# Attention, a dense MoE layer and a routed MoE layer in one kernel: gathers of later experts' tokens moved from the heads of two experts to the blocks of the experts before them

## The chip, the cores and the metric

The kernel runs on one core of one Trainium2 chip, as one launch. The metric is device time in microseconds (us) of that core; lower is better. The time quoted is the median of three runs. One further run was profiled, and all rows below come from it.

## The reference

Three stages follow each other over 2304 tokens (4 batches of 576) of width 512. Only the third is touched here.

```
x = attention(q, k, v)              # block-causal, 8 heads of 64, blocks of 64
x = elu(x @ w_in) @ w_out           # dense layer, 512 -> 2048 -> 512

skip_score = x @ w_skip             # routed layer, 8 experts
do_compute = skip_score > 0
out = x.copy()
xc = x[do_compute]
logits = xc @ w_gate
e_idx = argmax(logits)
gate_w = softmax(logits)[e_idx]
for e in range(8):
    mask = e_idx == e
    h = max(xc[mask] @ w1[e], 0)
    y[mask] = gate_w[mask] * (h @ w2[e])
out[do_compute] = xc + y
```

How many tokens an expert has is only known on the chip. Weights of an expert are w1 (512 x 1024) and w2 (1024 x 512).

## The kernel before

Attention and the dense layer are written through a recorder (class `Recorder`) that lays out the order of every engine by a list schedule; they end at about 604 us of the profiled execution and stay as they are. What follows is the routed layer, expert after expert.

**Tokens.** The router writes a list of token numbers per expert. A *gather* (`gather_to(e, j)`) fetches block j of expert e, 128 tokens: POOL issues an indirect DMA from `pay_d` into one of three staging buffers (two in tile `gp0`, one in tile `gp1`; they are used in turn, by the counter `ng`), and SP then issues a DMA transpose from there to the place that the matmuls read (`place_of`): a half of `mxt0`, `mxt1`, `mxwo2` or `mxwo6`. The next gather into a staging buffer has to wait until the transpose out of it has landed. A *scatter* adds a block's 128 result rows to `out`: ACT writes the rows to the tile `o` (two halves, used in turn by block), and POOL issues an indirect DMA from there.

**Blocks.** `block` computes one block on TensorE (PE): 96 matmuls into `hp`, ReLU and a split into high and low halves on ACT and DVE, 24 or 48 matmuls into `y`. The first block of small experts has 64 tokens instead of 128.

**Experts.** `ORDER` is 0, 6, 4, 5; `first_tokens` runs an expert's first block (its *head*), and `more_tokens` runs each further block inside a branch on the expert's count of tokens, each branch nested in the one before it. Every engine takes each branch for itself. Blocks past the fourth would run in a loop (`the_rest`). The four experts of `LAST` (1, 2, 3, 7) come at the end, their first blocks together in `last_tokens`. With the inputs of this kernel the blocks that run are: expert 0 one, expert 6 three, expert 4 three, expert 5 two, and one for each of 1, 2, 3, 7. Where a block does not run, its engines jump past its code to the next expert. The names E6 j2 and so on below mean expert 6, third block (j counts from 0).

**Weights.** The table `PREP` says what is done for later experts beside each block: `l` and `m` load half an expert's weights (four loads of 512 KB on SP's queue; `l` ahead of the block's own work, `m` later), `s`, `c` and `p` are steps of scaling and splitting on ACT and DVE. "4:l2-1 m7-0" loads w2 of expert 2 and w1 of expert 7 beside the head of expert 4.

**Which gathers stand where** (line 1710 and line 1793). The table `GATHERS` puts gathers behind an expert's first block, in the recording of its head; `more_tokens` puts more into the second block (j = 1), ahead of that block's own work. Before the change the head of expert 4 issues five gathers: its own third block, both blocks of expert 5 that will run, and the blocks of experts 1 and 2. The head of expert 5 issues three: its own third block and the blocks of experts 3 and 7. The second block of either expert issues one, for the fourth block.

POOL and SP work through their instructions in program order, so an instruction that waits holds up all that stand behind it.

Of the kernel before, what the change touches and what calls it, by code (L numbers as in the profile page):

```python
# [347 lines left out]
def tile_kernel(ctx, tc, q, k, v, w_in, w_out, w_skip, w_gate, w1, w2, out):  # L348
    nc = tc.nc
# [9 lines left out]
    NS = NT // 128 + 1  # L359
# [866 lines left out]
    for b in range(B):  # L1226
        g0, g1 = ubase[b, 0], ubase[b, 1]
# [191 lines left out]
        advance()  # L1419


    TM = 512

# [83 lines left out]
    def prep_steps(e, which, wait=0.0):  # L1509
        P_ = functools.partial  # L1510
        return ([("stat", P_(stat_w, e, which, x)) for x in range(4)] + [("scale", P_(scale_w, e, which, wait))]
                + [("split", P_(split_p, e, 4 * which + x)) for x in range(4)])
# [7 lines left out]
    def load_half(e, which, at=0.0):  # L1520
        for x in range(4):
            load_w(8 * e + 4 * which + x, at)
# [20 lines left out]
    def part(n, i32=False):  # L1543
        t = lists[:, off[0]:off[0] + n]
        off[0] += n
        return t.bitcast(I32) if i32 else t
# [3 lines left out]
    ni = part(17, True)  # L1550
# [42 lines left out]
    def gather(ix, xT):  # L1593
        gp = GP[ng[0] % 3]
        ng[0] += 1
        rc.gpsimd.indirect_dma_start(out=gp, out_offset=None, in_=pay_d[:, :],
                                     in_offset=bass.IndirectOffsetOnAxis(ap=ix, axis=0), bounds_check=NT - 1, oob_is_err=False)
        rc.sync.dma_start_transpose(out=xT, in_=gp.bitcast(F16))
# [89 lines left out]
    C0 = [int(any(x == e for x, _ in AHEAD)) for e in range(E)]  # L1688
# [3 lines left out]
    LAST = [1, 2, 3, 7]  # L1692
    XP = {0: 1, 6: 2, 4: 0, 5: 1}

    def place_of(e, j):
        if e in LAST:
            i = LAST.index(e)
            h = (X2[2 - i // 2 * 2], i % 2) if j == 0 else (X2[1], 1) if j == 1 else (X2[3], j % 2)
        else:
            h = X2[XP[e] if j < 2 else 3], j % 2  # L1700
        return h[0][:, :, 128 * h[1]:128 * h[1] + 128]

    def gather_to(e, j):
        gather(gix[:, e, C0[e] + j:C0[e] + j + 1], place_of(e, j))

    def pre_gather(e):
        for j in range(2):
            gather_to(e, j)

    GATHERS = {0: [], 6: [(6, 2), (4, 0), (4, 1)], 4: [(4, 2), (5, 0), (5, 1), (1, 0), (2, 0)], 5: [(5, 2), (3, 0), (7, 0)]}  # L1710

    PREP = {int(e): [x.split() for x in h.split("|")] for e, h in (y.split(":") for y in (
        "6:l1-1 m2-0 c5-0 p5-0 s1-0|c5-1 p5-1|c1-0 s1-1,4:l2-1 m7-0 p1-0 c1-1|p1-1 s2-0|c2-0 s2-1,"
        "5:l7-1 m3-0 p2-0 c2-1|p2-1,8:l3-1 s7-0 s7-1 c7-0 p7-0 c7-1 p7-1").split(","))}

    def aside_of(e, part):
        return PREP.get(e, [])[part:part + 1]
# [6 lines left out]
    def split_beside(e, part):  # L1724
        for h in sum(aside_of(e, part), []):
            if h[0] == "m":
                load_half(int(h[1]), int(h[3]), 5.0)
            if h[0] in "lm":
                continue
            for kind, f in prep_steps(int(h[1]), int(h[3]), 13.0 if e == 8 else 3.0):  # L1730
                if kind[1] == {"s": "t", "c": "c", "p": "p"}[h[0]]:
                    rc.atom()
                    rc.shift = -150000 if kind == "scale" else 0
                    f()
                    if h[0] == "s":
                        rc.ready[len(rc.steps) - 1] = 4.0
                    rc.shift = 0

    def tokens(e, j, xT, fs, par=None):

        c = C0[e] + j
        if j == 0 and e in SMALL:
            block(e, xT[:, :, 64:128], hix[:, e, c:c + 1], half[:, e, c, 1:2], j if par is None else par, 64)
        else:
            block(e, xT, six[:, e, c:c + 1], fs[:, c:c + 1], j if par is None else par)

    def first_tokens(e, fs):

        rc.begin()
        rc.late = rc.left  # L1750
        rc.urgent = True
        load_beside(e, 0)
        tokens(e, 0, place_of(e, 0), fs)
        rc.urgent = False
        for g in GATHERS[e]:
            gather_to(*g)
        split_beside(e, 0)
        rc.issue()

    def last_tokens():  # L1760

        rc.begin()
        rc.late = rc.left
        load_beside(8, 0)
        split_beside(8, 0)
        rc.urgent = True
        fs = {e: fac_w(e) for e in LAST}
        for i, e in enumerate(LAST):
            tokens(e, 0, place_of(e, 0), fs[e], i)
        rc.urgent = False  # L1770
        rc.issue()
        rc.left = {}
        with tc.If(cnt["last"] > 128, preferred_fallthrough_block=True, label="last"):  # L1773
            for e in LAST:
                read_count(e)
                more_tokens(e, 1, fs[e])

    def hint(e, j, n):

        tc.mark_branch_hint_location(f"n{e}_{j}", n > 128 * j, engines=[mybir.EngineType.PE])  # L1780

    def more_tokens(e, j, fs):

        aside = j and aside_of(e, j)
        now = rc.left
        keep = list(FREE), dict(RAW2), dict(WHL)
        with tc.If(cnt[e] > 128 * j, preferred_fallthrough_block=True, label=f"n{e}_{j}") as cmp:  # L1787
            if j < TM // 128:
                hint(e, j + 1, cnt[e])
                rc.begin()  # L1790
                rc.late = rc.left if j else {}
                rc.urgent = True
                for x in ((1, 2, 3) if e in LAST or e == 0 else (3,)) if j == 1 else ():
                    gather_to(e, x)
                tokens(e, j, place_of(e, j), fs)
                rc.urgent = False
                if aside:
                    split_beside(e, j)
                rc.issue()
                now = rc.left  # L1800
                more_tokens(e, j + 1, fs)

            else:
                the_rest(e, fs)
        if aside:
            with cmp.Else():
                FREE[:] = keep[0]
                for x, y in ((RAW2, keep[1]), (WHL, keep[2])):
                    x.clear()
                    x.update(y)  # L1810
                rc.begin()
                for part in range(j, len(PREP[e])):
                    split_beside(e, part)
                rc.issue()
        if j == 1:
            rc.left = now

    def the_rest(e, fs):

        trips = nc.values_load(ni[0:1, 8 + e:9 + e], min_val=TM // 128, max_val=NS)  # L1820
        sel = sm.tile([128, 3, NS], F32, tag="rw", bufs=1, name="sel")
        cj = sm.tile([128, 4], F32, tag="mx", bufs=4, name="cj")
        ci_ = sm.tile([128, 2], I32, tag="si", bufs=1, name="cji")
        nc.vector.memset(cj[:, 0:1], float(C0[e] + TM // 128 - 1))
        nc.gpsimd.iota(sel[:, 0], pattern=[[1, NS]], base=0, channel_multiplier=0, allow_small_or_imprecise_dtypes=True)
        with tc.For_i(TM // 128, trips):
            nc.vector.tensor_scalar(out=cj[:, 0:1], in0=cj[:, 0:1], scalar1=1.0, scalar2=None, op0=ALU.add)
            nc.vector.tensor_scalar(out=sel[:, 1], in0=sel[:, 0], scalar1=cj[:, 0:1], scalar2=None, op0=ALU.is_equal)
            for x, src in ((1, gix[:, e, :]), (2, six[:, e, :]), (3, fs)):
                nc.vector.tensor_tensor(out=sel[:, 2], in0=sel[:, 1], in1=src, op=ALU.mult)  # L1830
                nc.vector.tensor_reduce(out=cj[:, x:x + 1], in_=sel[:, 2], axis=AX.X, op=ALU.add)
            nc.vector.tensor_copy(ci_, cj[:, 1:3])
            gather(ci_[:, 0:1], X2[3][:, :, 0:128])
            block(e, X2[3][:, :, 0:128], ci_[:, 1:2], cj[:, 3:4], 0)
# [75 lines left out]
    with tc.manual_schedule():  # L1910
        for i, e in enumerate(ORDER):
            fs = fac_w(e)
            if i:
                hint(e, 1, cnt[e])
            first_tokens(e, fs)
            if i:
                read_count(ORDER[i + 1] if i + 1 < len(ORDER) else "last")
            n0 = ng[0]
            more_tokens(e, 1, fs)
            ng[0] = n0  # L1920
            FREE.extend(WHL.pop(8 * e + x) for x in range(8))
        tc.mark_branch_hint_location("last", cnt["last"] > 128, engines=[mybir.EngineType.PE])
        last_tokens()
# [23 lines left out]
```

## Time and profile before

| | us |
|---|---|
| median of three runs | 736.51 (735.89 to 737.37) |
| the profiled execution | 733.4 |
| its span, first to last instruction | 731.4 |
| expert 6, three blocks (604.25 to 637.01) | 32.8 |
| expert 4, three blocks (637.01 to 665.94) | 28.9 |
| expert 5, two blocks (665.94 to 687.78) | 21.8 |
| experts 1, 2, 3, 7 (687.78 to 721.2) | 33.4 |
| last scatter and end | 10.2 |

Starts of the stages are the first matmul of each in the timeline. PE is TensorE's matmul queue, PEld its weight loads, DVE VectorE, ACT ScalarE, POOL GpSimd, SP SyncE. "[2.61 <-issue]" behind a row means that the engine stood idle for 2.61 us before it and that the profile shows nothing that it waited for; with another name in its place, that instruction or DMA ended the wait. PEclk is TensorE's granted clock as a share of full speed. The median lies 3.1 us above the profiled execution, so a change worked out from the rows is added to the median.

### The profile page before, as it was taken

To read this page: it belongs to the slowest core of one execution; us is meant where nothing else is said; L and a number is where in the kernel's file an instruction comes from. 1 tells how busy PE (TensorE), PEld (TensorE's weight loads), DVE (VectorE), ACT (ScalarE), POOL (GpSimd) and SP (SyncE) were. 2 spreads that over 40 slices of the span, in tenths; PEclk is the share of its full clock that TensorE was granted. 3 is DMA by queue.
4 is the path that set the end of the run, shared out by engine and by line. 5 is a ranking of instruction groups with operands and counts; after the bars stand their busy time and mean duration, and the time that the engine had idled before them with its cause. 6 is when DMAs were issued, how large, how long until landed. Compare 5 with 4: busy or idle time off the path is not lost. (4 is left out here: it accounts for less than half of the span.)

```text
span 731.4 us, 17751 instructions
## 1 busy us (share of the span) xinstructions
PE 671.8 (92%) x6665; PEld 462.0 (63%) x6665; DVE 576.1 (79%) x1664; ACT 512.0 (70%) x1090; POOL 83.6 (11%) x122
## 2 busy tenths in 40 slices
PE   4669988999999999989999999999999999997994
PEld 3447633775476666647656757757576777675773
DVE  5887999987999999878969955999688655665552
ACT  5966746999987888677758745766466548695672
POOL 2000000001000000100100000100105034143312
PEclk9979999999999999999999999999999999999997
DMA  9999999898696999899538349826164787899941
GB/s 265 232 256 306 288 284 262 183 166 160 128 198 136 180 184 197 144 185 192 109 71 162 75 70 264 312 87 202 44 198 150 212 175 149 208 237 259 275 135 16
DMA packets 263259, 134.52 MB, mean 184 GB/s; under 512 B 234539, under 2 KB 235573, under 8 KB 262640
## 3 DMA queue, kind: packets, MB, share of 16 engines
q1 hardware_dynamic: 258960, 125.69, 74.7%
q0 software_dynamic: 4192, 7.49, 5.0%
q8 instruction: 57, 0.93, 0.6%
q14 instruction: 50, 0.41, 0.2%
HBM read 74.38 MB, written 12.75 MB: 119 GB/s over the span
## 5 line engine op out<-in xcount | busy, mean ns | idle before, releaser
L310 PE MATMUL h<-xt,win 128*128 128x256 f16 x1344 | 158.5, 273 | 1.6 <-DVE n L310 1.0
L310 PE MATMUL y<-wout,g 128*128 128x512 f16 x672 | 155.7, 379 | 0.0
L310 PEld LDWEIGHTS <-win 128*128 128x128 f16 x1344 | 128.9, 98 | 25.1 <-issue 2.8
L310 PEld LDWEIGHTS <-g 128*128 128x128 f16 x672 | 64.1, 98 | 66.6
L310 ACT ACTIVATE e<-s,mx 128x512 f32<-128x512 f32 (+4 forms) x160 | 82.3, 517 | 25.2 <-DVE mx L310 10.3
L310 ACT ACTIVATE ehl<-e,su 128x512 f16<-128x512 f32 (+4 forms) x160 | 80.5, 550 | 23.0 <-DVE su L310 10.2
L310 DVE SCALAR_TENSOR_TENSOR ehl<-e,su,ehl 128x512 f16<-128x512 f32 (+4 forms) x160 | 82.2, 540 | 10.8 <-ACT ehl L310 10.7
L310 DVE TENSOR_REDUCE mx<-s 128x1 f32<-128x512 f32 (+4 forms) x160 | 74.9, 476 | 5.6 <-PE s L310 5.2
L310 PE MATMUL s<-kt,qt 128*128 128x384 f16 (+5 forms) x384 | 70.0, 309 | 8.6 <-ACT e L310 6.6
L310 PE MATMUL h<-xt,twi 128*128 128x256 f32 x256 | 60.8, 391 | 3.2 <-ACT xt L310 2.3
L310 PE MATMUL xps<-et,vt 128*64 128x128 f16 (+1 forms) x1440 | 49.1, 217 | 13.5 <-DVE xt L310 3.0
L310 PE MATMUL y<-two,g 128*128 128x512 f32 x128 | 59.5, 603 | 1.6 <-DVE two L310 1.6
L310 PEld LDWEIGHTS <-vt 128*64 128x64 f16 x1440 | 39.5, 112 | 31.7 <-issue 23.8
L310 PEld LDWEIGHTS h<-xt,twi 128*128 128x128 f32 x256 | 48.5, 195 | 10.3 <-ACT xt L310 2.7
L310 ACT ACTIVATE el<-h,col 128x512 f32<-128x512 f32 x56 | 38.2, 682 | 23.7 <-PE h L310 22.7
L310 ACT ACTIVATE g<-el,col 128x512 f16<-128x512 f32 x56 | 40.1, 718 | 18.5 <-DVE el L310 18.2
L310 PEld LDWEIGHTS <-p 128*128 128x128 f16 x984 | 46.1, 98 | 9.8 <-PEq L1787 4.1
L310 PEld LDWEIGHTS <-qt 128*128 128x128 f16 (+1 forms) x384 | 28.7, 104 | 26.9 <-issue 11.5
L1506 DVE SCALAR_TENSOR_TENSOR p<-p,n,p 128x1024 f16<-128x1024 f32 x32 | 40.8, 1282 | 6.0 <-ACT p L1505 5.9
L310 DVE SCALAR_TENSOR_TENSOR g<-el,col,g 128x512 f16<-128x512 f32 x56 | 41.7, 745 | 3.9 <-ACT g L310 3.7
L310 DVE SCALAR_TENSOR_TENSOR el<-h,col,el 128x512 f32<-128x512 f32 x56 | 41.8, 746 | 1.3
L310 PEld LDWEIGHTS <-hh 128*64 128x64 f16 (+1 forms) x432 | 28.6, 106 | 21.0 <-issue 1.7
(233 smaller groups left out, 1131.2 us busy)
## 6 DMA issues: line engine op xcount, KB each, us to landing
p<-in_moe_w_dram SPq DMA_DIRECT2D x49, 512.0 KB, 6.1
rw<-in_moe_w_in_dram SPq DMA_DIRECT2D x16, 512.0 KB, 6.5
rw<-in_moe_w_out_dram SPq DMA_DIRECT2D x16, 512.0 KB, 4.5
pb<-in_moe_w_dram SPq DMA_DIRECT2D x10, 512.0 KB, 4.0
vflat<-in_v_dram SPq DMA_DIRECT2D x4, 1152.0 KB, 9.7
out_dram<-pay SPq DMA_DIRECT2D x18, 256.0 KB, 3.4
pay_d<-pay SPq DMA_DIRECT2D x18, 256.0 KB, 2.6
raw<-in_k_dram SPq DMA_DIRECT2D x16, 256.0 KB, 4.9
```

Of the source, the lines that this page charges most:

```text
L310: rec.call(e, time, lambda: getattr(self.real, op)(*args, **kw), reads, writes, dma)
L1506: rc.call("dve", 1.2, lambda: nc.vector.scalar_tensor_tensor(out=half(1), in0=raw.t, scalar=sc, in1=half(0), op0=ALU.mult, op1=ALU.subtrac ...
```

## The change

Expert 4's and expert 5's heads issue no gathers any more. Inside `PREP`, a new step `g` gathers: expert 5's two blocks beside E6 j1, experts 1 and 2 beside E6 j2, experts 3 and 7 beside E4 j2. The third blocks of experts 4 and 5 are gathered with the fourth at the start of their own second block (j = 1). Expert 0's branches get three blocks in line instead of four, its loop starts one block earlier, and its second block, which does not run here, would gather one block fewer. The number of gathers that run is the same, 14 from expert 6 on.

```diff
-    TM = 512
+    BLOCKS = [3] + [4] * 7
...
-    GATHERS = {0: [], 6: [(6, 2), (4, 0), (4, 1)], 4: [(4, 2), (5, 0), (5, 1), (1, 0), (2, 0)], 5: [(5, 2), (3, 0), (7, 0)]}
+    GATHERS = {0: [], 6: [(6, 2), (4, 0), (4, 1)], 4: [], 5: []}
...
-        "6:l1-1 m2-0 c5-0 p5-0 s1-0|c5-1 p5-1|c1-0 s1-1,4:l2-1 m7-0 p1-0 c1-1|p1-1 s2-0|c2-0 s2-1,"
+        "6:l1-1 m2-0 c5-0 p5-0 s1-0|g5-0 g5-1 c5-1 p5-1|g1-0 g2-0 c1-0 s1-1,4:l2-1 m7-0 p1-0 c1-1|p1-1 s2-0|g3-0 g7-0 c2-0 s2-1,"
...
-            if h[0] in "lm":
+            if h[0] == "g":
+                gather_to(int(h[1]), int(h[3]))
+            if h[0] in "lmg":
                 continue
...
-            if j < TM // 128:
+            if j < BLOCKS[e]:
...
-                for x in ((1, 2, 3) if e in LAST or e == 0 else (3,)) if j == 1 else ():
+                for x in {6: (3,), 4: (2, 3), 5: (2, 3), 0: (1, 2)}.get(e, (1, 2, 3)) if j == 1 else ():
                     gather_to(e, x)
...
-        trips = nc.values_load(ni[0:1, 8 + e:9 + e], min_val=TM // 128, max_val=NS)
+        trips = nc.values_load(ni[0:1, 8 + e:9 + e], min_val=BLOCKS[e], max_val=NS)
...
-        with tc.For_i(TM // 128, trips):
+        with tc.For_i(BLOCKS[e], trips):
```

On POOL, from the head of expert 4 to its second block, before the change. `gp0` and `gp1` are the staging tiles; a DMA into `out_0_dram` is a scatter (4608x256 is the one of a 64-token block, here E4 j0). The five gathers are those of expert 4's third block, of expert 5 (two), and of experts 1 and 2.

```order
L310 DMA gp0_1496<-pay_d_72,lists_1495 128x512 x2
L310 DMA gp1_1497<-pay_d_72,lists_1495 128x512
L1679 DMA out_0_dram<-o2_1505,gp1_1497 4608x256
L310 DMA gp0_1496<-pay_d_72,lists_1495 128x512 x2
L1883 TENSOR_LOAD lists_1495
L1787 COMPARE_AND_BRANCH
L310 DMA gp1_1497<-pay_d_72,lists_1495 128x512
L1679 DMA out_0_dram<-o2_1505,gp1_1497 2304x512
L1787 COMPARE_AND_BRANCH
```

The same place after it, to the end of the third block:

```order
L1679 DMA out_0_dram<-o2_1505,gp1_1497 4608x256
L1885 TENSOR_LOAD lists_1495
L1789 COMPARE_AND_BRANCH
L310 DMA gp0_1496<-pay_d_72,lists_1495 128x512 x2
L1679 DMA out_0_dram<-o2_1505,gp1_1497 2304x512
L1789 COMPARE_AND_BRANCH
L310 DMA gp1_1497<-pay_d_72,lists_1495 128x512
L310 DMA gp0_1496<-pay_d_72,lists_1495 128x512
L1679 DMA out_0_dram<-o2_1505,gp1_1497 2304x512
L1789 COMPARE_AND_BRANCH
```

The gather of expert 4's third block stood ahead of the scatter of E4 j0 and stands behind it and behind the branch now.

On SP, the same stretch before the change, from the last of the loads for expert 2 on. `mxwo6` is the place of expert 4's third and fourth blocks, `mxt1` that of expert 5's, `mxwo2` that of experts 1 and 2; `p1` to `p4` are the weights of expert 7.

```order
L310 DMA_TRANSPOSE mxwo6_1504<-gp0_1496 128x8x128
L310 DMA_TRANSPOSE mxt1_1502<-gp0_1496 128x8x128
L310 DMA_TRANSPOSE mxt1_1502<-gp1_1497 128x8x128
L1455 DMA p1_7186<-in_moe2_w1_dram 128x1024
L1455 DMA p2_7187<-in_moe2_w1_dram 128x1024
L1455 DMA p3_7188<-in_moe2_w1_dram 128x1024
L1455 DMA p4_7189<-in_moe2_w1_dram 128x1024
L310 DMA_TRANSPOSE mxwo2_1503<-gp0_1496 128x8x128 x2
L1883 TENSOR_LOAD lists_1495
L1883 ISA x2
L1787 COMPARE_AND_BRANCH
L310 DMA_TRANSPOSE mxwo6_1504<-gp1_1497 128x8x128
```

And after it (`mxt0` is the place of experts 3 and 7):

```order
L1458 DMA p0_7185<-in_moe2_w2_dram 128x2x512
L1455 DMA p1_7186<-in_moe2_w1_dram 128x1024
L1455 DMA p2_7187<-in_moe2_w1_dram 128x1024
L1455 DMA p3_7188<-in_moe2_w1_dram 128x1024
L1455 DMA p4_7189<-in_moe2_w1_dram 128x1024
L1885 TENSOR_LOAD lists_1495
L1885 ISA x2
L1789 COMPARE_AND_BRANCH
L310 DMA_TRANSPOSE mxwo6_1504<-gp0_1496 128x8x128 x2
L1789 COMPARE_AND_BRANCH
L310 DMA_TRANSPOSE mxt0_1441<-gp1_1497 128x8x128
L310 DMA_TRANSPOSE mxt0_1441<-gp0_1496 128x8x128
```

The loads of expert 7 follow those of expert 2 directly, the transpose for E4 j2 stands behind all eight, and the two transposes for experts 1 and 2 have left this stretch: they stand in E6 j2, ahead of the eight loads.

## Rows read from the trace of the kernel before

**Rows 1.** The page: busy time of each engine, and the packets of instruction queue q8.

```profile
PE 671.8 (92%) x6665; PEld 462.0 (63%) x6665; DVE 576.1 (79%) x1664; ACT 512.0 (70%) x1090; POOL 83.6 (11%) x122
...
q8 instruction: 57, 0.93, 0.6%
```

**Rows 2.** Windows: experts 6, 4, 5, last; busy per engine, clock, DMA share, GB/s.

```profile
604.25:637.01 32.76, 31.87 (x363) 23.15 (x364) 20.12 (x45) 24.67 (x47) 10.01 (x7) 1.00 0.79 182
637.01:665.94 28.93, 27.47 (x386) 20.57 (x387) 18.25 (x38) 23.14 (x43) 11.89 (x9) 1.00 0.91 248
665.94:687.78 21.84, 17.00 (x265) 12.90 (x266) 13.27 (x24) 13.47 (x22) 8.39 (x6) 1.00 1.09 238
687.78:721.20 33.42, 31.90 (x514) 26.55 (x514) 17.65 (x38) 22.39 (x40) 7.45 (x4) 1.00 0.51 148
```

**Rows 3.** Timeline of PE: start, length, tiles, count, idle time before and its end.

```profile
637.01 2.96 PE L310 MATMUL hp<-mxt,p 128*128 128x64 f16 x96 [0.90 <-ACTq L1787]
...
643.77 5.53 PE L310 MATMUL hp<-mxt,p 128*128 128x128 f16 x96
...
654.33 4.18 PE L310 MATMUL hp<-mxwo,p 128*128 128x128 f16 x72
...
665.94 0.42 PE L310 MATMUL hp<-mxt,p 128*128 128x64 f16 x9 [0.89 <-ACTq L1787]
...
670.52 0.36 PE L310 MATMUL hp<-mxt,p 128*128 128x64 f16 x7 [2.61 <-issue]
...
674.90 1.28 PE L310 MATMUL y<-pb,hh 128*64 128x256 f16 x20 [1.00 <-DVE n L310]
676.12 0.68 PE L310 MATMUL hp<-mxt,p 128*128 128x128 f16 x9
...
695.69 0.92 PE L310 MATMUL y<-pc,hh 128*64 128x256 f16 x13 [1.47 <-issue]
```

**Rows 4.** Timeline of POOL: three gathers (third blocks of 4, expert 1, third of 5).

```profile
644.96 1.08 POOL L310 DMA_INDIRECT gp<-pay_d,lists  x1 [6.28 <-DMA out_dram<-o,gp]
...
654.39 1.04 POOL L310 DMA_INDIRECT gp<-pay_d,lists  x1 [2.85 <-DMA mxwo<-gp]
...
674.28 1.12 POOL L310 DMA_INDIRECT gp<-pay_d,lists  x1 [6.64 <-DMA mxwo<-gp]
```

**Rows 5.** The chain of waits: scatter of E6 j2, start and time to landing.

```profile
637.12 6.92 DMA out_dram<-o,gp
```

**Rows 6.** Timeline of SP, issue of transposes and of expert 7's first loads.

```profile
649.45 1.26 SPq L310 DMA_TRANSPOSE mxwo<-gp  x1
...
654.06 2.00 SPq L1455 DMA_DIRECT2D p<-in_moe_w_dram  x4
661.14 8.63 SPq L310 DMA_TRANSPOSE mxwo<-gp  x3
...
680.50 1.27 SPq L310 DMA_TRANSPOSE mxwo<-gp  x1
...
692.60 2.03 SPq L310 DMA_TRANSPOSE mxwo<-gp  x1
```

**Rows 7.** Timeline of ACT: E4 j0's result rows written for the scatter.

```profile
644.15 0.47 ACT L310 ACTIVATE o<-y,gp 128x256 f32<-128x256 f32 x1 [0.86 <-DMA out_dram<-o,gp]
```

**Rows 8.** Tiles mxwo and gp, 600 to 732 us: transposes' landing; scatters' issue, gathers' and scatters' landing.

```profile
DMA to landing us min/median/max: 4.2/4.7/7.0
...
L1679 POOL DMA_INDIRECT out_dram<-o,gp x13: 1552/1627/2383, 604.4 to 721.9; - x13
...
DMA to landing us min/median/max: 3.1/5.6/8.7
```

**Rows 9.** Windows around two idle times of PE; columns as in rows 2.

```profile
48.00:51.00 3.00, 0.74 (x4) 0.59 (x4) 1.58 (x5) 1.60 (x5) 0.00 (x0) 1.00 1.29 251
51.00:55.00 4.00, 4.00 (x13) 3.21 (x12) 4.00 (x9) 3.60 (x7) 0.00 (x0) 0.57 1.00 355
...
668.00:672.00 4.00, 1.48 (x39) 1.20 (x38) 1.54 (x3) 1.60 (x4) 0.00 (x0) 1.00 1.30 145
```

More of the change, by code (lines that the diff above doesn't have):

```diff
@@ L1823, in the_rest @@
         ci_ = sm.tile([128, 2], I32, tag="si", bufs=1, name="cji")
-        nc.vector.memset(cj[:, 0:1], float(C0[e] + TM // 128 - 1))
+        nc.vector.memset(cj[:, 0:1], float(C0[e] + BLOCKS[e] - 1))
         nc.gpsimd.iota(sel[:, 0], pattern=[[1, NS]], base=0, channel_multiplier=0, allow_small_or_imprecise_dtypes=True)
-        with tc.For_i(TM // 128, trips):
+        with tc.For_i(BLOCKS[e], trips):
             nc.vector.tensor_scalar(out=cj[:, 0:1], in0=cj[:, 0:1], scalar1=1.0, scalar2=None, op0=ALU.add)
```

## Prediction, made before the changed kernel was run

> **What bounds the kernel now.** I read the page first, then the windows by expert, then PE's timeline where the windows show idle time, and last the queues that PE waits for there. The page has PE busy for 671.8 us of 731.4 [rows 1], and the windows say the same of the routed layer: PE is busy for all but 0.9 us of expert 6, 1.5 us of expert 4 and 1.5 us of the last four, but idle for 4.8 of 21.8 us in expert 5 [rows 2]. So a gather or a load costs time only where PE runs dry because of it, and expert 5 is where there is something to win.
>
> PE's timeline puts expert 5's idle time in its first block: 0.89 us for the jump, 2.61 us that end with "issue", and 1.00 us for DVE after that [rows 3]. E5 j0 takes 665.94 to 676.12, 10.2 us; the same 64-token block of expert 4 takes 637.01 to 643.77, 6.8 us [rows 3]. The difference, 3.4 us, is all that expert 5's head can give back.
>
> What is in flight during that "issue" wait? SP issues three transposes from 661.14 on, over 8.63 us [rows 6], and from 668 to 672 the DMA engines are taken up fully (share 1.30) for only 145 GB/s, against 355 GB/s at a share of 1.00 around 53 us [rows 9]: small packets. The other wait of this kind, 1.47 us before 695.69 [rows 3], comes while the transpose issued at 692.60 is in flight [rows 6]. The heads of experts 6 and 4, with loads in flight but no transpose, show none [rows 2, 3]. The engine waits for nothing that has a semaphore, and instructions come by DMA too (queue q8, 57 packets of 16 KB each) [rows 1]; I take it that PE ran out of instructions behind the transposes' packets, soon after a jump.
>
> **The third block of expert 4.** This is the part that costs. Before, its gather goes out at 644.96, ahead of E4 j0's scatter [rows 4], and its transpose at 649.45 [rows 6]. The next gather into that staging buffer, at 654.39, waited for that transpose [rows 4]; POOL needs 0.92 us from a landing to the gather's start (scatter landed at 637.12 + 6.92 = 644.04, gather at 644.96 [rows 4, 5]), so the transpose landed near 653.5. PE begins E4 j2 at 654.33 with no wait [rows 3]: the old order had 0.8 us to spare.
>
> In the new order the gather stands behind the scatter of E4 j0 and a branch. Step by step: ACT writes the rows until 644.15 + 0.47 = 644.62 [rows 7]; it starts no sooner, since it waits there for the landing of E6 j2's scatter (644.04) [rows 5]. POOL takes up the scatter some 0.3 us later and spends the median of 1.63 us on it [rows 8]: 646.5. With 0.92 us for the branch and the registers, the gather starts at 647.45, 2.5 us later than now. Its landing takes 3.1 to 8.7 us (median 5.6) [rows 8]. I take 6.2, as for the gather of 674.28, whose transpose went out at 680.50 with four weight loads in flight [rows 4, 6]: eight loads are in flight here, since those of expert 7, now issued at 654.06 behind the transposes [rows 6], move up to just behind those of expert 2. So the transpose goes out at 653.65. It lands 4.2 to 7.0 us later, median 4.7 [rows 8]: 658.35. PE wants it at 654.33 [rows 3]. **Cost: 4.0 us**, between 0.4 (both least values: 654.75) and 8.8 (both greatest: 663.15). Nothing hides it, since E4 j2's matmuls read this place and PE has no other work; ACT and DVE catch up on their preparation of weights meanwhile, which is not on the path.
>
> An idle time of that length also brings the clock into play. After PE stood nearly idle from 48 to 51 us, the granted clock was 0.57 on average over the next 4 us, so partly at 1.2 GHz; over the 2.6 us before 670.52 and behind them it stayed at 1.00 [rows 3, 9]. Four idle microseconds are more than either. At 0.57, 4 us of PE's time lose 0.43 x 4 = **1.7 us**; the other end is 0, as at 670.5.
>
> **Expert 5's head.** The three transposes that ran into it move: those of experts 1 and 2 to E6 j2, that of expert 4's fourth block to just behind the third's. In their place stand two, for experts 3 and 7, gathered behind E4 j1's scatter. With E4 j2 4 us late, these two have landed before expert 5 begins. The 2.61 us go, and some of the 1.00 us behind them, which came of DVE being held up by the same stall: **gain 3.0 us**, between 0 (the wait belongs to the jump, or comes back) and 3.4.
>
> **Parts taken at nothing.** The four gathers moved into E6 j1 and j2 lie beside 21 us of unbroken matmuls [rows 2]; POOL and SP have room, since POOL is busy for 10 of 33 us there [rows 2]. On SP they stand ahead of the loads for expert 2, which so go out some 5 us later; ACT and DVE need those in E4 j2 and the loads of expert 7 only in the last stage. If the cover were gone, E6 j2's scatter would go out late, and E4 j0's rows, already waiting 0.86 us for it [rows 7], with it. The transposes of experts 1 and 2 will now be in flight while expert 4 begins: by the pattern of the two "issue" waits this can cost PE 0 to 2.6 us there; I take 0. Expert 5 ran dry 670.52 - 2.61 - 665.94 = 1.97 us after its first matmul [rows 3]; for expert 4 that is 639.0, and the first of these transposes will hardly have gone out by then: its gather has to wait for the transpose of E6 j1's, and then takes its own 5.6 us [rows 8]. At the last four experts two transposes are in flight instead of one: between -1.5 and +1.1 us around the 1.47 of now, taken at 0. The shorter code of expert 0 is jumped over as before; jumps cost about 0.9 us whatever their length [rows 3]: 0.
>
> **Sum.** 4.0 + 1.7 - 3.0 = +2.7 us. Against the profiled execution's own time that is 733.4 + 2.7 = 736.1; against the median of the runs, which lies 3.1 above it, 736.5 + 2.7 = **739.2 us**. What this kernel's measurements can tell from no change is about 0.2%, 1.5 us.
>
> **Rivals.**
>
> *The gather is quick.* If the new gather and its transpose both come near their least values, E4 j2 waits 0.4 to 1.5 us, the clock stays up, and expert 5's 3.0 to 3.4 us are kept, with up to 1.5 more at the last experts: about -2.3, 734.2. For it: this gather landed within 4.5 us before (644.96 to 649.45 [rows 4, 6]). Against it: the loads of expert 7 were still unissued then. It turns faster when gather and transpose together take under about 8.8 us (a wait of 1.5 us, half the gain). Chance 0.20.
>
> *The two cancel.* Gather and transpose take 9 to 10 us, the wait is 2 to 3.5 us, short enough for the clock to stay at 1.00 as at 670.5 [rows 9], and expert 5 gives 3.0 back: within 1.5 us of 736.5. Chance 0.22.
>
> *The jump is the price.* PE's 2.61 us may hang on the jump into expert 5 alone and not on the transposes; the jump stays. Then nothing is gained, and the wait and the clock stand alone: +5.7, 742.2, and more if expert 4's head catches a stall as well (up to 745). For it: both "issue" waits come soon after a jump. Against it: the jumps into experts 6 and 4 show none [rows 2, 3]. Chance 0.13. The Trainium skill, "Runtime: NRT & Kernel Launch", section "Instruction fetch mechanics", says that a taken branch to code outside the window at hand forces a fetch of that page before execution goes on. By that rule alone every jump would stall alike; in this trace two of four do, so I give it no more.
>
> *The forecast*, slower by 1.5 to 8 us: 0.45.
>
> That the change might not do what it says I leave out: the order of POOL and SP shows the gathers in their new places.
>
> **How the numbers follow.** Slower by over 0.2%: 0.45 + 0.13 = 0.58; within 0.2%: 0.22; faster: 0.20. The likeliest case gives 739.2. All bounds together reach from 736.5 + 0.4 - 3.4 - 1.5 = 732.0 to 736.5 + 8.8 + 1.7 + 2.6 + 1.1 = 750.7. The range leaves out some 0.12 below and 0.06 above: 734.0 to 744.5; the forecast's own range is 738.0 to 744.5.
>
> **What would show it.** Right: an idle time of 2.5 to 6 us on PE just before E4 j2's first matmul, ended by the DMA into mxwo; a granted clock under 1.00 in the microseconds after it; expert 5's first block at about 7 us without an "issue" wait; POOL's gather for E4 j2 near 647 and SP's transpose near 654. Wrong: E4 j2 starting with no wait although its gather went out later (then gathers land faster than I took), or the 2.61 us standing in expert 5's head as before, or stalls of that kind in expert 4's head, which would carry all of expert 4 back with it.

## The result, and the profile after

The changed kernel takes **743.2 us** (740.4 to 743.5, six runs) against 736.6 us (735.8 to 737.4) for the kernel before beside it: a ratio of 1.0083, 95% interval 1.0066 to 1.0099. It is slower, by 6.6 us. On a second chip the ratio was 1.0067 (1.0031 to 1.0103). The first profiled execution of the changed kernel took 743.27 us, with a span of 741.5 us.

Windows by expert, as [rows 2]: length, busy time of each engine, granted clock, DMA share, GB/s.

```profile
606.61:639.37 32.76, 31.87 (x364) 23.16 (x365) 20.05 (x45) 24.68 (x47) 14.29 (x11) 1.00 0.89 223
639.37:675.58 36.21, 30.11 (x386) 22.98 (x387) 18.24 (x38) 23.26 (x43) 9.46 (x7) 0.91 0.85 212
675.58:695.46 19.88, 17.15 (x266) 12.75 (x267) 13.08 (x24) 13.37 (x22) 5.78 (x4) 1.00 1.00 277
695.46:731.20 35.74, 33.53 (x514) 27.76 (x514) 17.64 (x38) 22.39 (x39) 7.48 (x4) 0.95 0.29 77
```

Beside [rows 2], expert 6 has its 32.76 us as before, expert 4 grows by 7.28 us, expert 5 shrinks by 1.96, and the last four grow by 2.32. Two of the four stages now show a clock under 1.00. The sum is +7.64 us. A further 2.36 us lie ahead of expert 6 (606.61 against 604.25), a stretch that moves by 5 us and more between traces of one and the same code, as the table below shows.

PE's timeline says where in the stages, as in [rows 3]: start, length, tiles, count, idle time before it and what ended that.

```profile
661.49 6.66 PE L310 MATMUL hp<-mxwo,p 128*128 128x128 f16 x72 [4.65 <-DMA mxwo<-gp]
...
675.58 0.42 PE L310 MATMUL hp<-mxt,p 128*128 128x64 f16 x9 [0.89 <-ACTq L1789]
...
679.01 0.41 PE L310 MATMUL y<-pb,hh 128*64 128x256 f16 x4 [0.47 <-ACT hh L310]
680.42 1.50 PE L310 MATMUL y<-pb,hh 128*64 128x256 f16 x24 [1.01 <-DVE hh L310]
...
683.29 0.68 PE L310 MATMUL hp<-mxt,p 128*128 128x128 f16 x9
...
703.96 1.88 PE L310 MATMUL y<-pc,hh 128*64 128x256 f16 x18 [1.99 <-issue]
```

E4 j2 waits 4.65 us for the transpose into `mxwo`, where before it started at 654.33 with no wait. Its first 72 matmuls then take 6.66 us instead of 4.18. The jump into expert 5 still costs 0.89 us, but the 2.61 us behind it are gone. In the last four experts PE waits 1.99 us for its instructions, against 1.47.

The order of POOL and SP around the third block of expert 4, beside [rows 4] and [rows 6]:

```profile
646.99 1.83 POOL L1679 DMA_INDIRECT out_dram<-o,gp  x1 [5.88 <-ACT o L310]
649.13 1.08 POOL L310 DMA_INDIRECT gp<-pay_d,lists  x1 [0.30 <-issue]
...
646.03 2.38 SPq L1455 DMA_DIRECT2D p<-in_moe_w_dram  x4
657.17 3.07 SPq L310 DMA_TRANSPOSE mxwo<-gp  x2
```

The gather goes out at 649.13, behind the scatter, and its transpose 8.04 us later. The four loads for expert 7 went out ahead of both (646.03). From the transpose to PE's first matmul (661.49) are another 4.32 us.

What the two long idle times do to the clock, in windows with the columns of [rows 9]:

```profile
660.00:667.00 7.00, 5.51 (x55) 5.54 (x56) 0.42 (x1) 0.99 (x3) 2.26 (x3) 0.52 0.83 171
...
704.00:708.00 4.00, 4.00 (x65) 3.48 (x66) 0.00 (x0) 0.66 (x3) 1.37 (x1) 0.57 0.08 26
```

After 4.65 idle us PE works at 0.52, close to 1.2 GHz, until 667; after 1.99 it works at 0.57 for 4 us.

### The profile page after: what moved, and what is told of

Same layout as the page of the kernel before. It is cut to its first block, busy times and chain, and to the rows that moved or that the text cites. A ratio compares the mean times of both kernels' runs of the same rounds, so it can differ in the third digit from the quotient of the medians.

```text
span 741.5 us, 17760 instructions
## 1 busy us (share of the span) xinstructions
PE 676.5 (91%) x6665; PEld 465.8 (63%) x6665; DVE 576.2 (78%) x1664; ACT 512.6 (69%) x1090; POOL 83.2 (11%) x122
## 5 line engine op out<-in xcount | busy, mean ns | idle before, releaser
L310 PEld LDWEIGHTS <-p 128*128 128x128 f16 x984 | 49.3, 102 | 12.9 <-issue 6.5
```

The source lines that it names most:

```text
L310: rec.call(e, time, lambda: getattr(self.real, op)(*args, **kw), reads, writes, dma)
```

## The experiments

All are edits of the changed kernel, except where the kernel before is named. They ran on several chips, and each ratio is to the kernel before on the same chip. The spread on these was wider than in the first comparison (the kernel before: 732.8 to 748.5 us), so beside the ratios I read the stages of each trace, cut at the first matmul of each stage. The issue waits given are those behind a jump; single ones of 0.15 to 0.36 us inside E6 j0, E4 j2 and E5 j1 are left out.

| trace | start of E6 | E6 | E4 | E5 | last four | E6 to last | wait before E4 j2 | issue waits: E4 / E5 / last four |
|---|---|---|---|---|---|---|---|---|
| before, first | 604.25 | 32.76 | 28.93 | 21.84 | 33.42 | 116.95 | 0 | 0 / 2.61 / 1.47 |
| before_again | 605.08 | 32.77 | 29.34 | 20.51 | 32.70 | 115.32 | 0 | 0.50 / 1.34 / 0.63 |
| before_third | 610.85 | 32.76 | 30.28 | 22.58 | 33.85 | 119.47 | 0 | 0 / 3.25 / 0.77 + 1.01 |
| after, first | 606.61 | 32.76 | 36.21 | 19.88 | 35.74 | 124.59 | 4.65 | 0 / 0 / 0.22 + 1.99 |
| after_again | 606.75 | 32.81 | 36.29 | 19.76 | 35.64 | 124.50 | 4.95 | 0 / 0 / 1.99 |
| e1_42_at_head | 607.65 | 34.08 | 29.77 | 20.72 | 35.78 | 120.35 | 0.43 | 0 / 1.28 / 1.47 + 0.88 |
| e1_again | 606.29 | 33.48 | 30.61 | 19.97 | 31.76 | 115.82 | 0 | 0 / 0 / 0 |
| e2_loads_behind | 609.09 | 34.71 | 29.93 | 19.98 | 38.69 | 123.31 | 0.16 | 0 / 0 / 1.81 + 2.81 |
| e3_12_early | 607.48 | 32.75 | 31.49 | 21.68 | 37.50 | 123.42 | 0 | 2.12 / 0.18 / 2.68 + 1.11 |
| e4_no_g52_g53 | 605.75 | 34.61 | 34.27 | 19.91 | 32.76 | 121.55 | 3.19 | 0 / 0 / 0.67 |
| e7_42_head_5_head | 606.09 | 32.77 | 29.30 | 23.76 | 35.24 | 121.07 | 0.22 | 0 / 3.63 / 1.80 + 1.45 |
| e8_loads_behind_5_head | 604.96 | 32.76 | 29.91 | 19.56 | 33.52 | 115.75 | 0.74 | 0 / 0 / 1.44 |
| e8_again | 606.55 | 33.73 | 29.83 | 21.21 | 33.52 | 118.29 | 0 | 0 / 0 / 1.44 |
| e11_idle_copies | 607.59 | 32.76 | 35.22 | 23.56 | 31.90 | 123.44 | 4.50 | 0 / 0.99 / 0 |

### The third block of expert 4 back at the head

```
-    GATHERS = {0: [], 6: [(6, 2), (4, 0), (4, 1)], 4: [], 5: []}
+    GATHERS = {0: [], 6: [(6, 2), (4, 0), (4, 1)], 4: [(4, 2)], 5: []}
...
-    for x in {6: (3,), 4: (2, 3), 5: (2, 3), 0: (1, 2)}...
+    for x in {6: (3,), 4: (3,), 5: (2, 3), 0: (1, 2)}...
```

> The changed kernel with one part undone: the third block of expert 4 is gathered at the head of expert 4 again, ahead of that expert's first scatter and of the loads for expert 7; all other gathers stay where the change put them. Theory (the late gather is the price): the wait of 4.65 us ahead of E4 j2 goes, with it the half clock behind it (E4 j2 10.7 us again and not 13.2), together 7.1 us, and the head of expert 5 stays without its 2.61 us: 743.2 - 7.1 = about 736, which is level with the kernel before, or below it by up to 2. Rival one (expert 5 was only helped by expert 4 being late): the two transposes for experts 3 and 7 now run into E5 j0, an issue wait of 1 to 3 us comes back there: 738 to 739. Rival two (the wait has another cause, say the transposes' own packets): E4 j2 still waits over 2 us for the DMA into mxwo: 741 to 743.

Measured: 736.56 us, ratio to the kernel before (742.12 us on this chip) 0.9938 (0.9908 to 0.9968). PE's timeline and, in the last row, SP's:

```profile
659.82 4.18 PE L310 MATMUL hp<-mxwo,p 128*128 128x128 f16 x72 [0.43 <-DMA mxwo<-gp]
...
674.70 0.26 PE L310 MATMUL hp<-mxt,pb 128*128 128x64 f16 x3 [1.28 <-issue]
...
673.88 2.87 SPq L310 DMA_TRANSPOSE mxt<-gp  x2
```

The wait before E4 j2 falls from 4.65 to 0.43 us, its 72 matmuls take 4.18 us again, and expert 4 takes 29.77 us. So expert 4's loss hangs on this one part of the change. The edit moves more than the gather, though: the four loads for expert 7 now go out behind its transpose, at 657.75, 16.0 us after expert 4's start and not 6.7. Which of the two counts, this run alone does not tell. Rival one is half right as well: with expert 4 no longer late, an issue wait of 1.28 us is back in expert 5's head (running since 671.50). But the wait begins at 673.42, before the two transposes for experts 3 and 7 go out (673.88), so they can't have begun it. What fills the DMA engines then is queue q0, which carries POOL's gathers and scatters: 83.4% of them from 669 to 672.2.

### Only the loads for expert 7 later

```
-    "...,4:l2-1 m7-0 p1-0 c1-1|p1-1 s2-0|g3-0 g7-0 c2-0 s2-1,"
+    "...,4:l2-1 p1-0 c1-1|p1-1 s2-0|g3-0 g7-0 m7-0 c2-0 s2-1,"
```

> The changed kernel with the four loads of the first half of expert 7's weights moved from the head of expert 4 to behind the transposes for experts 3 and 7, so that fewer loads are in flight while the third block of expert 4 is gathered (the gather itself stays as late as the change made it). Theory (order and traffic both): gather and transpose together took 12.2 us behind the loads (649.13 to about 661.4); without four of the loads they take 8 to 10, E4 j2 waits 0.5 to 2.5 us, the clock stays up: 738 to 741. Rival one (order alone): the landing takes as long as before, the wait stays at 4 to 5 us and the time at 743. Rival two (traffic alone): the wait vanishes, 736 or less.

Measured: 740.81 us, ratio 0.9989 (0.9952 to 1.0027). Timelines of PE, POOL and SP:

```profile
662.11 4.18 PE L310 MATMUL hp<-mxwo,p 128*128 128x128 f16 x72 [0.16 <-DMA mxwo<-gp]
...
653.70 1.08 POOL L310 DMA_INDIRECT gp<-pay_d,lists  x1 [0.30 <-issue]
...
658.73 2.65 SPq L310 DMA_TRANSPOSE mxwo<-gp  x2
```

The gather is as late in its stage as in the changed kernel (9.9 us behind expert 4's start; there 9.8), yet PE waits only 0.16 us: gather and transpose together take 8.4 us at most (653.70 to 662.11), against 12.4 (649.13 to 661.49). So for expert 4 the rival "traffic alone" holds: it is the loads ahead of it that make the late gather a wait. The time does not follow: the last four experts take 38.69 us, with issue waits of 1.81 and 2.81. The displaced loads have moved what comes after them; the transposes for expert 5's last two blocks now go out from 692.15 to 698.14, across the jump (first matmul at 693.71).

### The kernel before, with the gathers of experts 1 and 2 beside E6 j2

```
-    4: [(4, 2), (5, 0), (5, 1), (1, 0), (2, 0)]
+    4: [(4, 2), (5, 0), (5, 1)]
...
-    "6:l1-1 m2-0 c5-0 p5-0 s1-0|c5-1 p5-1|c1-0 s1-1,..."
+    "6:l1-1 m2-0 c5-0 p5-0 s1-0|c5-1 p5-1|g1-0 g2-0 c1-0 s1-1,..."
```

> The kernel before with one part of the change: the gathers for experts 1 and 2 go out beside E6 j2 and not at the head of expert 4; everything else stays. So the three transposes that stood in the queue when expert 5 began are fewer and earlier. Theory (PE ran dry in E5's head because its instructions stood behind the transposes' packets): the 2.61 us of issue wait go, E5 j0 takes about 7 us and not 10.2, no new wait elsewhere: 736.6 - 3 = 733 to 734. Rival (the jump is the price): E5 j0 still has an issue wait of 2 to 3 us with no transpose in flight, and the time stays at 736 to 737.

Measured: 738.96 us, ratio 0.9952 (0.9926 to 0.9979), 3.2 us under the 742.12 of the kernel before on this chip. PE's timeline, and SP's in the last row:

```profile
644.85 0.74 PE L310 MATMUL hp<-mxt,p 128*128 128x64 f16 x20 [2.12 <-issue]
...
673.97 0.36 PE L310 MATMUL hp<-mxt,p 128*128 128x64 f16 x7 [0.18 <-issue]
...
637.01 7.53 SPq L310 DMA_TRANSPOSE mxwo<-gp  x3
```

The 2.61 us in expert 5's head shrink to 0.18 with the jump where it was, so the jump alone is not the price. But the transposes, now issued from 637.01 to 644.54, span the jump into expert 4 (first matmul at 640.23), and there a wait of 2.12 us appears that the first trace of before does not have. The wait moved with them. This trace (743.15 us) is the longest of the kernel's ten runs, so it shows where a wait can go, and not why the median lies below the kernel before.

### No gathers for expert 5's third and fourth blocks

```
-    for x in {6: (3,), 4: (2, 3), 5: (2, 3), 0: (1, 2)}...
+    for x in {6: (3,), 4: (2, 3), 5: (), 0: (1, 2)}...
```

> The changed kernel without the two gathers of expert 5's third and fourth blocks beside E5 j1; they are left out altogether, which these inputs never use (expert 5 has two blocks here). Theory (the issue wait of 1.99 us in the first of the last four experts and the half clock behind it come of those two transposes, issued at 691.56, being in flight behind a jump): both go, the stage of the last four experts takes 32 to 33 us and not 35.75: 743.2 - 3 = about 740. Rival (the wait is the jump's, or comes of the next loads): it stays at 1.5 to 2 us, 742.5 to 743.5.

Measured: 741.23 us, ratio 1.0008 (0.9974 to 1.0043). The last four experts in PE's timeline:

```profile
701.33 1.25 PE L310 MATMUL y<-pc,hh 128*64 128x256 f16 x19 [0.67 <-issue]
```

and in the window of that stage:

```profile
694.54:727.30 32.76, 31.93 (x514) 26.43 (x514) 17.71 (x38) 22.30 (x40) 7.40 (x4) 1.00 0.31 81
```

The stage takes 32.76 us instead of 35.74, at a clock of 1.00: as expected, though 0.67 us of waiting stay with no transpose in flight. So in the changed kernel these two transposes carry most, but not all, of what the last stage lost. How they do it is not shown: their small packets are through by 697 (from 697 to 701.6 only 46 of 830 packets have under 512 bytes), and the wait of 1.99 us begins at 701.97, when weight loads are in flight.

### The two kernels themselves, once more

> The changed kernel itself, unchanged, on this chip, to stand beside the experiments: stages from expert 6 to the last four of 34.6, 34 to 36, 19.9 and 35 to 36 us; a wait of 3 to 5 us for the DMA into mxwo ahead of E4 j2. If expert 6 takes 32.8 us and not 34.6, the 0.3 us issue wait and the wait for DVE behind it in that stage vary from run to run; if it takes 34.6, they belong to this chip. Ratio to the kernel before: 1.00 to 1.01.

> The kernel before itself, for a second trace of it on this chip. If the issue waits hang on what is in flight, they stand at the same places (1.97 us of work behind the jump into expert 5, 6.4 us behind the jump into the last four) with other lengths; if they are fixed costs, 2.6 and 1.5 us as in the first trace. Expert 4 without a wait for the DMA, 28.9 to 31 us.

The changed kernel: 743.74 us, ratio 1.0067. Its trace repeats the first almost exactly (table). The kernel before, PE's timeline:

```profile
670.50 0.36 PE L310 MATMUL hp<-mxt,p 128*128 128x64 f16 x7 [1.34 <-issue]
...
694.78 0.93 PE L310 MATMUL y<-pc,hh 128*64 128x256 f16 x13 [0.63 <-issue]
```

Both waits stand before the same matmuls as in [rows 3] (x7 and x13 follow), and at the same distance from the jump: 670.50 - 1.34 - 667.19 = 1.97 us, as in the first trace; 694.78 - 0.63 - 687.70 = 6.45, there 6.44. Only the lengths differ, 1.34 for 2.61 and 0.63 for 1.47. The places are fixed, the lengths are not. The 1 to 2 us by which expert 6 was longer in three of the first four experiments did not show in either kernel here; I could not settle where that came from.

### Both third blocks at their heads

To the first experiment's edit: `5: [(5, 2), (5, 3)]` in `GATHERS`, and `5: ()` beside the second block.

> The changed kernel with the third block of expert 4 gathered at the head of expert 4, as in the first experiment, and also the third and fourth blocks of expert 5 at the head of expert 5 and not beside its second block, so that no transpose is in flight at the jump into the last four. Theory: that stage falls from 35.8 to about 32.8 us, expert 4 stays at 29.8 and expert 5 at 20.7: 3 us under the first experiment, 733 to 734, ratio to the kernel before 0.990. Rival (the stall moves with the transposes into the second block of expert 5, as the experiment with experts 1 and 2 showed 2.2 us there): expert 5 takes 22 to 23 us, 735 to 736.

Measured: 737.63 us, ratio 0.9988 (0.9955 to 1.0022). PE's timeline, then SP's:

```profile
673.62 0.34 PE L310 MATMUL hp<-mxt,pb 128*128 128x64 f16 x3 [3.63 <-issue]
...
695.22 0.23 PE L310 MATMUL hp<-mxwo,pd 128*128 128x64 f16 x2 [1.80 <-issue]
...
670.01 3.78 SPq L310 DMA_TRANSPOSE mxt<-gp  x2
```

A miss on both counts. The transposes for experts 3 and 7 (670.01 to 673.79) fall right onto the place 1.83 us behind the jump, and PE waits 3.63 us there, longer than in any trace of before. The wait begins at 669.99, just before the first of them goes out; from 667 to 670.1 it is q0 again, with 85.0% of the DMA engines, so their gathers and a scatter come first here too. And the last four wait 1.80 and 1.45 us although the last transposes went out from 680.86 to 686.31: by then only weight loads are in flight (issued from 686.35 and from 691.83). So the transposes are not the only traffic that does it.

### Loads later, and expert 5's blocks at its head

The second experiment's edit, with `5: [(5, 2), (5, 3)]` in `GATHERS` and `5: ()` beside the second block.

> The changed kernel with the loads for expert 7 behind the transposes for experts 3 and 7, as in the second experiment, and the third and fourth blocks of expert 5 gathered at the head of expert 5. Theory: expert 4 without a wait (29.9 us) though its gather stays late, the head of expert 5 free (20 us) since its transposes landed before, the last four 33 us and not 38.7: 5 us under the second experiment, about 735, ratio 0.992. Rival (the delayed loads, now in one heap behind the jump into expert 5, hold up the gathers and the next instructions there): expert 5 takes 22 us or more, or the last four over 35, and the time stays at 738 to 741.

Measured: 737.91 us, ratio 1.0007 (0.9972 to 1.0043). Windows of experts 4, 5 and the last four:

```profile
637.72:667.63 29.91, 27.63 (x386) 20.50 (x387) 18.33 (x38) 23.10 (x43) 9.39 (x7) 1.00 0.78 176
667.63:687.19 19.56, 16.98 (x265) 12.83 (x266) 12.94 (x24) 13.36 (x22) 5.43 (x4) 1.00 1.09 296
687.19:720.71 33.52, 32.00 (x514) 26.53 (x514) 17.68 (x38) 22.38 (x39) 7.39 (x4) 1.00 0.45 145
```

The stages came out as the theory has it: expert 4 at 29.9 us with the late gather, expert 5 at 19.6. With the same late gather as the changed kernel, this one is level with the kernel before, so the mechanism of the loss is undone. The gain did not follow: a ratio of 0.992 was expected.

### Added copies over the jump into expert 5

Nothing is left out. Behind the order of SP in E4 j2:

```
+    if (e, j) == (4, 2):
+        for x in range(8):
+            i = rc.call("sp", 0.48, lambda x=x: nc.sync.dma_start(out=idle_d[128 * x:128 * (x + 1), :], in_=w1[x // 4][...]), [], [], 1.46)
+            rc.ready[i] = 8.0
```

> The changed kernel with eight added copies of 512 KB each from one place in DRAM to another that nobody reads, issued behind the transposes for experts 3 and 7 in expert 4's third block, so that they are in flight over the jump into expert 5; PE's instructions and their order stay the same. No transpose is in flight there. Theory (PE's next instructions come late whenever the DMA engines are full at that place): an issue wait of 1 to 3 us appears about 1.9 us of work behind the jump into expert 5, where the changed kernel has none; expert 5 takes 21 to 23 us and not 19.8. Rival (only the small packets of the transposes do it): no issue wait there, expert 5 stays at 19.8 to 20 us, and later loads are merely late. The stages ahead of expert 5 as in the changed kernel.

Measured: 743.08 us in one run. PE's timeline, and SP's:

```profile
678.38 0.26 PE L310 MATMUL hp<-mxt,pb 128*128 128x64 f16 x3 [0.99 <-issue]
...
669.97 5.07 SPq L1804 DMA_DIRECT2D idle_d<-in_moe_w_dram  x8
```

The window of the last four:

```profile
699.13:731.03 31.90, 31.82 (x514) 26.48 (x514) 17.71 (x38) 22.27 (x39) 7.48 (x4) 1.00 0.49 101
```

With PE's own order unchanged, a wait of 0.99 us appears 678.38 - 0.99 - 675.57 = 1.82 us behind the jump, where neither trace of the changed kernel has one. Copies in large pieces suffice (from 672.3 to 677 their queue moves 1.51 MB in 92 packets), so the small packets are not needed; that is one trace. The wait is at the low end of what I expected; the rest of expert 5's growth to 23.56 us is other waits (1.24 us for ACT and 0.75 us for DVE among them). And in the last four, transposes issued at 699.05 with little else in flight cost nothing.

### The best version again, and a third trace of before

> The first experiment once more (third block of expert 4 gathered at that expert's head, the rest as changed), since its time (0.994 of the kernel before) and its trace (experts 6 to the last four 120.4 us, against 115.3 and 117.0 in the two traces of the kernel before) point opposite ways. If the time tells what is typical: ratio again 0.991 to 0.997. If the trace does: 1.000 to 1.005, with an issue wait of 1 to 3 us in the head of expert 5 and again in the last four.

> The kernel with the loads for expert 7 behind the transposes for experts 3 and 7 and the third and fourth blocks of expert 5 gathered at the head of expert 5, once more, beside the first experiment on one chip. Its trace had experts 6 to the last four at 115.8 us, its ratio was 1.0007 (0.997 to 1.004). Theory (the head of expert 5 is free in all its runs): 0.995 to 1.000, and under the first experiment. Rival (the issue wait in the last four eats the gain): 1.000 to 1.005.

> The kernel before once more, for a third trace beside these two. If its two traces (733.4 us each) were typical by their stages, experts 6 to the last four take 115 to 117 us again; if their low times were luck, the issue waits behind the jumps are longer here and that stretch takes 118 to 121 us.

Measured: the first experiment's kernel 735.43 us, ratio 0.9947 (0.9921 to 0.9974); the other 739.25, ratio 0.998 (0.9946 to 1.0013). So **leaving the third block of expert 4 at its head and making the other moves beats both kernels**: about 0.6% under the kernel before on both chips, 4.4 and 5.6 us by the medians. The other one stayed above it. The third trace of before, PE's timeline:

```profile
679.13 0.36 PE L310 MATMUL hp<-mxt,p 128*128 128x64 f16 x7 [3.25 <-issue]
```

Here the wait is 3.25 us and the whole run 742.8 us: the two traces of 733.4 us were lucky ones. The three traces of before lost 4.08, 2.47 and 5.03 us in issue waits behind the jumps into experts 4, 5 and the last four, the two of the best version 3.63 and 0. On average that is some 2 us. But the traces do not carry the gain: expert 6 to the last four take 117.2 us on average in the three traces of before and 118.1 in the two of the best version, so where its 4 to 6 us lie stays open.

## Why the prediction was right, and where its sizes were off

The direction was right, and the measured 743.2 us lie inside the range, at its upper end, 4.0 us over the forecast. By stages the sum of +2.7 us met +7.6 in the traces.

- **The wait before E4 j2, forecast 4.0, measured 4.65 and 4.95.** Right in place and size, half right in cause. Its parts were off in opposite directions: counted from expert 4's start the gather went out 9.8 us later (forecast 10.4), it took 8.0 us to the transpose (6.2), and that took 4.3 (4.7). The 8.0 lie inside the bound of 8.7 that [rows 8] gave. I had named the eight loads in flight as the reason for taking more than the median; the traces show that they are not a correction but nearly the whole wait. Counted from expert 4's start, the transpose goes out at 17.4 to 17.8 us in the four traces with the loads for expert 7 ahead of it, and at 14.0 to 14.9 in the six traces of its variants without them there. In three of those six the gather stands at the head and goes out at 5.7 to 7.1 us, in the other three it stands behind the scatter and goes out at 9.8 to 10.1, and that makes no difference: the transposes go out at 14.4 to 14.7 and at 14.0 to 14.9, and PE waits 0 to 0.43 us and 0 to 0.74. So the step that failed inside this term is the gather's later start (2.5 us in the forecast): it cost 0.7 us at most, where the forecast without its 1.7 us for the loads (6.2 against 4.5) would still have had a wait of 2.3. That the total came out right is in part luck.
- **The clock, forecast 1.7, measured 2.5.** E4 j2 up to the jump takes 13.20 us (661.49 to 674.69) instead of 10.72. The mechanism held. The size came from a window of 4 us in [rows 9]; here the half clock lasted until 667.
- **The head of expert 5, forecast -3.0, measured -2.0** (against the first trace of before). The 2.61 us went, and "the jump is the price" fell: the jump's 0.89 us stayed without them. What I got wrong is the 1.00 us for DVE: I took it for a consequence of the stall, but it stands there without one (1.01), and a wait of 0.47 us for ACT comes to light beside it. So j0 gave back 2.47 us (10.18 to 7.71); the second block lost 0.51. The sentence that the two new transposes "have landed before expert 5 begins" because E4 j2 is late was right, and the two kernels with the third block of expert 4 back at its head show its price: without that lateness the gathers for experts 3 and 7, and the transposes behind them, ran into expert 5's head, with waits of 1.28 and 3.63 us, though in one trace of three they cost nothing.
- **The last four experts, forecast 0 (-1.5 to +1.1), measured +2.3.** This is the term that failed most, outside its own bounds. Two transposes instead of one made 1.99 us of 1.47, but also pulled the clock down: 4 us at 0.57, some 1.7 us. I priced the clock only where I expected the long wait. The fourth experiment takes away the half clock and all but 0.67 us of the waits: 32.76 us. It is not a fixed price: in the second trace of the best version two transposes go out across this jump (689.17 to 691.85), and nothing waits.
- **"Instructions stand behind the transposes' packets."** Half right. That PE waits for instructions is borne out by the list of DMA packets in the traces: in each of the 27 issue waits of the table, PE goes on 1.2 to 2.4 us after a packet of 16 KB of queue q8 has landed, in 25 of them 1.2 to 1.65 us. In the first trace of before that packet moves from 668.00 to 669.08, and PE goes on at 670.52. In expert 5's head the packet starts 2.06, 0.74 and 1.85 us behind the jump in the three traces of before, which wait there; it starts 2.46 and 2.42 us ahead of the jump in the two of the changed kernel, which do not, and 0.51 behind it with the added copies, which do. But transposes are not needed for it: gathers and scatters (the two kernels with expert 4's third block at its head), weight loads (the last four with both third blocks at their heads) and plain copies were in flight at other such waits. What holds the packet up before it starts, no row shows, and the same kernel had waits of 1.28, 1.47 and 0.88 us in one trace and none in another. The Trainium skill, "Runtime: NRT & Kernel Launch", section "Instruction fetch mechanics", says that instructions come in blocks of 16 KiB by a DMA queue of the engine's own and that crossing a block's end is mostly hidden. The 57 packets of 16 KB in [rows 1] agree with the first half. The second holds here away from jumps: of the 16 packets between 604.25 and 721.2 in the first trace of before, two end an issue wait, both behind a jump. There it does not hold, with waits of up to 3.63 us.
- **Parts at nothing.** Expert 6 took 32.76 us as forecast, expert 4's head showed no issue wait, and the shorter code of expert 0 left no trace that can be told from the spread: the wait for that jump was 0.82 to 1.78 us with the old code and 0.80 to 1.83 with the new.

The rival "the gather is quick" put its turning point at 8.8 us for gather and transpose, and called that a wait of 1.5 us; by its own start at 647.45 and PE's need at 654.33 it is 1.9, and 1.5 belongs to 8.4. They took 12.4. The experiment that brought them down to 8.4 removed the wait, as that rival says, but did not become faster than the kernel before (0.9989): the last four experts lost what expert 4 had won.

## What to carry to other kernels

When a gather is moved behind another step, look at what is moved ahead of it in the same queues: here the later place alone cost 0.7 us at most, and with four loads issued in front of it 3.2 to 5. Traffic taken off one jump can land on the next, so follow every moved transfer to the jump that it will now be in flight over. And price the clock at every wait that may reach 1.5 us, not only at the longest one.

## What the hardware showed unexpectedly

- The issue waits stand at fixed places: 2.4 to 2.5 us of work behind the jump into expert 4 (two traces), 1.8 to 2.1 behind the jump into expert 5, 1.5 to 1.65 and 6.1 to 6.6 behind the jump into the last four (the second of these read from the traces whose clock stayed up until there). Their length runs from 0 to 3.63 us, and differs more than twofold between traces of the same kernel (1.34, 2.61, 3.25). Each ends 1.2 to 2.4 us after a 16 KB packet of q8 has landed.
- The length of the idle time alone does not say whether the clock falls. It stayed at 1.00 behind 2.61 us in expert 5 [rows 9], but fell behind 1.99 us in the last four of both traces of the changed kernel, and behind 1.47 us in the last four of the first experiment (0.61 over the 4 us from 695.19).
